# Feed-forward rows transposed by DMA instead of TensorE, in a two-layer recurrent-memory transformer kernel

## The chip, the core and the metric

The kernel runs on one core of a Trainium2 chip. A core has a matrix engine (TensorE, PE in the profile; its weight loads are PEld), three elementwise engines (VectorE or DVE, ScalarE or ACT, GpSimd or POOL) and SyncE (SP), whose queue issues most DMAs. The metric is the device time of one execution in microseconds.

## The reference

The input is one sequence of 2048 rows of 576 numbers. Two layers are applied, and each is attention with a recurrent memory followed by a gated feed-forward; both layers use the same weights.

```python
x = x + _A_ref(_layernorm(x), mem0, Wq, Wk, Wv, Wo, 32)
x = x + _B_ref(_layernorm(x), w1, w3, w2)
# the same two lines once more
def _A_ref(...):            # 64 segments of 32 rows, 32 heads of 128
    for s in range(n_seg):
        h = concatenate([mem, xs])            # 8 memory rows and 32 rows
        q, k, v = h Wq, h Wk, h Wv
        o = softmax(mask(q k^T * scale)) v    # per head
        o = o Wo
        mem = o[:, :8]                        # the next segment needs this
        outs.append(o[:, 8:])
def _B_ref(x):  return (silu(x w1) * (x w3)) w2    # 4608 hidden columns
```

The memory makes the attention of a layer a chain of 64 segments. Layer norm is taken over a row's 576 numbers.

## The kernel before

**Steps and jobs.** A step t works on segment t of layer 0 and on segment t - 8 of layer 1 together, where both exist; there are 72 steps. Four segments make a group of 128 rows. When a group of a layer has gone through attention, a feed-forward job (`job`, L460) takes it: the job of one point in time holds a group of layer 0 and a group of layer 1, two blocks of 128 rows. Its hidden columns are worked in 18 slices, whose weights (W13, W2C) are loaded from memory anew for each job.

**A step on PE.** Queries and keys (QK, and QKt for the last 64 of the 576 numbers), values (VX, VM, VG), scores (SC), the transposed probabilities times the values (PV), and the output projection (WO, WOt). Between scores and PV lie the mask's addition (`sm_add`), the maximum, the exponential on ACT, the sum and the normalised probabilities PB. With both layers at work PB is transposed into PTS by a DMA (`ptr_dma`, L1046, on SP); with one layer, in the first and last eight steps, PE does it (`ptr`). There is one PTS buffer. The last WO tails are spread over two halves of the partitions; `y_odd` (L1112) copies the second half to YO on ACT, and `y_mem` and `yts` add the first half to it, for the next step's memory rows and for YTS, the attention's output with the 576 numbers across partitions.

**A job's entry.** `post_tr` (POST) turns a group of YTS back into rows with five PE transposes, `post_add` adds them to XR on DVE, `ln_nodes` (L277) takes the layer norm: statistics on DVE, the power on POOL, the normalised rows XN on DVE (`ln_norm`, L792). `ln_tr` (L802) transposes XN on PE, each 128 columns as two half-array matmuls, and `xtb_write` (L844) copies the bank to XTB on ACT or DVE. The feed-forward's up matmuls (FF and FFt) read XTB. The same `ln_nodes` serves the attention's inputs (L0tr, L1tr), whose transposes go to HT instead.

**Who sets the order.** PE's order is written out: one letter a PE step, in `FIRST`, eleven times `FOUR`, and `LAST` (L201 to L222). A turn of `FOUR` is four steps and one two-block job. `plan` (L78) walks the steps with assumed durations, follows the letters on PE and places the steps of the other engines and of SP's queue where their inputs and buffers (POOLS, L38: eight PSUM banks among them) let them start. What it decides is the order on each engine; each engine then runs its instructions in that order and waits on semaphores.

**Array divisions.** A PE step uses the array whole (128 x 128), in column halves or quarters (128 x 64, 128 x 32) or in row halves (64 x 128 and smaller). `plan` picks between whole and column halves where a step allows both. The tails of 64 rows (QKt, FFt, VGt and the like) use row halves.

```python
            for c in range(5):
                for r in (0, R64):
                    c0 = min(c * P + r, D - R64)
                    self.mm(self.lnps(b)[r:r + R64, c, :], self.T.XN[:, xn.i, c0:c0 + R64], self.T.ident[:, 0:P], True, True,
                            is_transpose=True, tile_position=(0, r))
```

These are the ten matmuls of `ln_tr`; the tenth block of 64 columns is the ninth again, so that XTB's last block holds the last 64 numbers on both halves of the partitions.

Of the kernel before, what the change touches and what calls it, by code (L numbers as in the profile page):

```python
# [13 lines left out]
P = 128  # L14
# [22 lines left out]
NOW = 1.0e18  # L37
POOLS = {"bank": 8, "qkt": 4, "sme": 2, "pb": 2, "pts": 1, "ot": 4,  # L38
# [157 lines left out]
def ewh(*ns):  # L196
# [5 lines left out]
    "amqQqQQSqqQSqQTQQqqSqQSxXVvPTPTOPOoToPOOooQQqqqqQSQvqSQVqQQqQSTqSPTXPOTOPToxoPOOooQQqqqvaSVQQqqQSQqTQPSqQqOSoTPO"  # L202
    "TPTPOOoooQQQqqqqQSvSVqqqQQQTSQqPTSOPXTOPTxooPOOooQQpQqqVvqqSnQQSFfqFQqfqqQTQSPFTSfWPOOoofTFPFTOPofOoWQqqqqQQSQQS"
    "FFffqVvqqWQQSTFxqffQFPSXWTFfPOTOPoofTOPFOooWVqfqvQQFSQqqQFSQqfqQWTSQqfPFQTfqFPSOTWPOOFoTooffPFOoWQQqqqqQSvQVSFqf"
    "QqQWqqSQTQPTaOPbSOTxxoPXoTXPOOoovqqpQQQSnQFqfqVSFqfqQQQqSPfqFQfOPSWOPFoOfoFoPWOoFQfqqqQQSQfqFFSGqfgqQQQPWQfqqSFG"
    "SfggGPFOOPWoGogfOPFOooWQQqqfaFSVfqqFQQvqfFSQWQfqqFPSQQWqfOSPFFOoPoWOoffFPOoWQqqqqQQbSQGSQqqgqQQSQqgPGSOPGggOPGOo"
    "PooOoQqqqpQpQQSvqqQSnnVqffFFQQPSqfqFQFSPWwffOFOPwWooFPOOooFqffqQQQqqwWSFQQQqfqfFSGSgqqQQgPGwGPWSggfFOGPOwFPOOooo"
    "oWQqfqqQQQfqSFSVvqqfQQFFPWSfqqQwQFSPaffOwWFPOFOPWOwfooooFfqqQQWQqqSQQqqSbQGgqqSQQgPGSGPGggOPOwOPoooOo"
)
FOUR = (  # L210
    "QQppQqqqqQvVSnnSQFqqfqQQFSqffQPFwOSPWFoffPOFOWwPFOoooFfqfqQQQQqqSWGSFqqfgQQQPQgqqwSGSFPGffggFWGPOwOFPOOoooowVqfq"
    "vQQQQqfqWSFSFfqqqQQwWQFPfqfSFwQOPSWFoFPffOOWPwOoooFqqfQQWQSqqqQQaSbQQqgqqGSQgPGSGPGggOPOwOPoooOo"
)
LAST = (
    "QqqqpQQQSnpQQqqqVvSnSQfqFFPqfQOWPSwoFffOPFoOFPwOffWooFQQQqqqFQSqffqFQQqgSWGSQPwQqqgfGSFPFgfgGwOPOGOPWOffooooFQQq"
    "qqFSQQqqqVSvQQwWQSPFqfqQOWoPSwFFPffOOWPwOoooFvfqQQQqqqQSVSFfqqfQFQQqqSPWQwSOPVovWPOwOPoobOoXxvppVqqQQQqqSQQnSnqq"
    "QFQSTfqfqQPFSTOPFTOPWTOPwOooooFfqqfQQQSQQqqqVvTSQFQqffqqFSQPwTWPSFfOFTwPOTWPOOooooFqfqfQQQwSQqxvqfXVWSFQFTQfqqWP"
    "wQSTFQfqfqFPSOTwPWFOffOTFPwOoooWoFfqqvVQQQqfqSQWwSFFQfqqQQSTWPQqqOTSoPTOPwOToboPxOoXqqqQQQpSVvqqqQQnSQFTfSFQPfqq"
    "QOTSFfPwOTFPofTOPFOooowQQfqqqQSQFvfqqVSQFfqQQSqfqQTwPFSTFPOTfXxPOTwPOOooooFVqqfvQQQSQqfqqQSQFqqqQSQTwPFTSOPoffTO"
    "FPwTOPoofOoFQQvqqQSQqqVSQqqqQqQSTQPTSPFOOTffooPFTOPwOoopFffFwnwFffffFFFwFwfffFFFwfffFFwFwfffFFFwffFFwfffFFww"  # L220
# [11 lines left out]
def make_nodes(em, nseg, pools, o=Opt, dma_bw=230e3, load_bw=345e3):  # L232
# [44 lines left out]
    def ln_nodes(tag, src, xn, deps, prio, writes, warm=False):  # L277

        a = node("DVE", 1.16, em.ln_stats(src, xn), deps=deps, prio=prio, acq=[] if src is xn else [xn], name=tag + "stats")
        p_ = node("POOL", 0.45, em.ln_pow(xn), deps=[a], prio=prio, name=tag + "pow")  # L280
        c = node("DVE", 0.43 if src is xn else 0.6, em.ln_norm(src, xn), deps=[p_], prio=prio, name=tag + "norm")
        b = Slot("bank", users=len(writes))
        d = node("PE", 5 * 0.056, em.ln_tr(xn, b, warm), deps=[c], prio=prio, mode="col", acq=[b], rel=[xn], name=tag + "tr")
        out = []
        for wr, cost, more in writes:
            out.append(node("AD", cost, wr(b), deps=[d] + more + out[-1:], prio=prio, rel=[b], name=tag + "wr"))
        return out
# [20 lines left out]
    vx_ev, last_v, pvs = {}, [], {}  # L308

# [45 lines left out]
    def step(t):  # L355
# [17 lines left out]
        for g in range(NG):  # L373
# [27 lines left out]
            if nl == 2:  # L401
                tr = node("DMA", 1.27, em.ptr_dma(t, g, pb, pts), deps=[pbs], prio=pf - 0.02, acq=[pts], name="TR", lat=2.0)
# [31 lines left out]
        yo = node("ACT", actc(c80), em.y_odd(t), deps=wots[3:], prio=t - 0.008, name="Yodd")  # L434
# [10 lines left out]
    def post(li, g):  # L445

        b = banks(1)
        prio = 4 * g + 4 + LAG * li
        d = node("PE", 5 * 0.056, em.post_tr(li, g, b[0]), deps=[d for j in range(4) for d in yx[li, 4 * g + j]] + ([xr_ld[g]] if li == 0 else []),
                 prio=prio, mode="full/col", acq=b, name="POST")  # L450
# [9 lines left out]
    def job(j):  # L460
# [19 lines left out]
        def norm():  # L480
            for (bi, g, half) in reversed(ents):
                pa = post(bi, g)
                wr.extend(ln_nodes("F", xr[g], Slot("xn"), [pa], s0, [((lambda half: lambda b: em.xtb_write(half, b))(half), cost, prev_ff)], last))
# [113 lines left out]
class Emitter:  # L597
# [116 lines left out]
    def load_xn(self, g, xn):  # L714
        return lambda n: (self.dma if g else self.adma)(self.T.XN[:, xn.i, :], self.a.x[g * P:(g + 1) * P, :])
# [57 lines left out]
    def src_ap(self, src):  # L773
        return self.T.XN[:, src.i, :] if src.pool == "xn" else self.T.XR[:, src.i, :]
# [17 lines left out]
    def ln_norm(self, src, xn):  # L792
        def f(n):
            L = self.T.LNS[:, xn.i]
            self.v("tensor_scalar", self.T.XN[:, xn.i, :], self.src_ap(src), L[:, 12:13], L[:, 15:16],
                   op0=ALU.subtract, op1=ALU.mult)
        return f
# [4 lines left out]
    def ln_tr(self, xn, b, warm=False):  # L802

        def f(n):
            for _ in range(10 if warm else 0):
                self.mm(self.bk(b)[:], self.T.ident[:, 0:P], self.T.WO[:, 0, 0:512], True, True)
            for c in range(5):
                for r in (0, R64):
                    c0 = min(c * P + r, D - R64)
                    self.mm(self.lnps(b)[r:r + R64, c, :], self.T.XN[:, xn.i, c0:c0 + R64], self.T.ident[:, 0:P], True, True,  # L810
# [559 lines left out]
```

## Time and profile before

| | us |
|---|---|
| median of three runs (2652.61 to 2658.91) | 2656.71 |
| the profiled execution | 2657.08 |
| its span | 2655.3 |
| PE busy | 2577.3 (97%) |
| DVE busy | 2042.0 (77%) |
| ACT busy | 1226.3 (46%) |
| one turn of the repeated order, from the trace | 152 to 156 |

In the profile a row of a group names the line of the recording helper, the engine, the operation, what it writes and reads, the shape, the count, and then busy time, the mean duration of one in ns, and the idle time of the engine before it with what ended it. L620 is PE's helper, L623 ACT's, L626 DVE's, so the tiles tell the steps apart. "128*64" on a matmul is the part of the array that it uses. A row of the waits gives the total in us, how many, and the longest. A timeline row starts with the start and the duration in us. A matmul's duration covers its way through the array, some 0.2 us, and matmuls overlap; the work is read from the distance of their starts. "->" and "<-" name the tile written and the tiles read.

### The profile page before, as it was taken

The numbers are of one execution on the slowest core, as the hardware profiler recorded it, in microseconds if no ns is written. First come the engines' busy times: TensorE is split into PE (matmuls) and PEld (weight loads), VectorE is DVE, ScalarE is ACT, GpSimd is POOL, SyncE is SP. The second block draws the span as 40 slices with busy tenths as digits, with TensorE's granted clock in tenths as the row PEclk, the third lists the DMA queues.
The fourth block names the chain that finished last, engine by engine and source line by source line (L and its number), as shares of the span: only waits on it lengthen the run. The fifth ranks groups of instructions, "written<-read, shape, count | busy, mean of one in ns | idle before, by whom it ended". The sixth has DMA issues, their size and how long they took to land.

```text
span 2655.3 us, 132788 instructions
## 1 busy us (share of the span) xinstructions
PE 2577.3 (97%) x58915; PEld 2226.7 (84%) x58915; DVE 2042.0 (77%) x5253; ACT 1226.3 (46%) x3636; POOL 334.9 (13%) x399
## 2 busy tenths in 40 slices
PE   5999999999999999999999999999999999999998
PEld 4788888888888888888888888888888888888887
DVE  4787787787787778778777787787878777787876
ACT  2555453443445444444544444454534435454453
POOL 1111110110111011011101101110110111011110
PEclk8999999999999999999999999999999999999999
DMA  9064745665665556556454645645464564454456
GB/s 322 4 175 126 194 104 147 126 136 146 128 141 109 142 133 146 139 125 155 117 135 118 161 128 133 158 117 132 116 154 126 134 162 103 127 124 129 128 167 227
DMA packets 683056, 371.44 MB, mean 140 GB/s; under 512 B 233736, under 2 KB 672656, under 8 KB 681840
## 3 DMA queue, kind: packets, MB, share of 16 engines
q1 hardware_dynamic: 678944, 355.07, 52.9%
q8 instruction: 460, 7.54, 1.2%
q0 software_dynamic: 3024, 6.93, 0.9%
q10 hardware_dynamic: 512, 0.94, 0.2%
q14 instruction: 116, 0.95, 0.1%
HBM read 306.72 MB, written 2.36 MB: 116 GB/s over the span
## 4 chain that ended last, share of the span: by engine, by line
PE 83%; DMA 8%; DVE 5%; issue 1%; ACT 1%; SPq 1%; POOL 0%; ACTq 0%; DVEq 0%; POOLq 0%
PE bank L620 83%; DMA PTS<-PB 6%; DVE V L626 1%; DVE STAT L626 1%; DMA W<-in_B_w_dram 1%; DVE HTT L626 1%; DVE PB L626 1%; DVE SME L626 1%; DMA W<-in_A_Wk_dram 1%; SPq L629 1%; DMA W2C<-in_B_w_dram 1%; POOL PB L1041 0%; DMA WV<-in_A_Wv_dram 0%; DVE XR L626 0%; ACT V L623 0%
## 5 line engine op out<-in xcount | busy, mean ns | idle before, releaser
L620 PEld LDWEIGHTS <-W 128*128 128x128 bf16 (+2 forms) x31872 | 1254.5, 100 | 138.0 <-issue 68.5
L620 PE MATMUL bank<-HT,W 128*128 128x80 bf16 (+3 forms) x23040 | 804.6, 197 | 23.1 <-DMA W<-in_A_Wk_dram 8.7
L620 PE MATMUL bank<-XTB,W 128*64 128x256 bf16 (+5 forms) x8832 | 666.8, 263 | 2.5 <-DMA W<-in_B_w_dram 2.0
L1041 POOL MEMSET PB<- 128x1024 bf16 x288 | 274.1, 952 | 1954.7 <-DMA PTS<-PB 1298.5
L623 ACT ACTIVATE QKT<-bank 128x256 bf16<-128x256 f32 (+4 forms) x1546 | 356.3, 315 | 298.1 <-PE bank L620 287.2
L620 PE MATMUL bank<-OT,WO 128*128 128x80 bf16 (+3 forms) x11520 | 413.8, 198 | 1.2 <-ACT OT L623 0.6
L620 PEld LDWEIGHTS <-WO 128*128 128x128 bf16 (+1 forms) x11520 | 385.2, 102 | 26.4 <-issue 13.5
L623 ACT ACTIVATE V<-bank 64x512 bf16<-64x512 f32 (+1 forms) x583 | 328.9, 584 | 129.7 <-PE bank L620 122.5
L620 PE MATMUL bank<-WV,HT 128*32 128x512 bf16 (+3 forms) x3952 | 376.4, 386 | 1.2 <-DVE HT L626 0.7
L620 PE MATMUL bank<-W2C,HTT 128*64 128x288 bf16 (+1 forms) x3032 | 319.1, 287 | 1.3 <-DMA W2C<-in_B_w_dram 1.1
L623 ACT ACTIVATE HTT<-bank 128x512 bf16<-128x512 f32 (+1 forms) x324 | 175.7, 551 | 274.6 <-PE bank L620 273.4
L623 ACT ACTIVATE OT<-bank 128x320 bf16<-128x320 f32 (+1 forms) x378 | 142.2, 402 | 314.9 <-PE bank L620 312.1
L626 DVE TENSOR_REDUCE STAT<-SME 104x8 f32<-104x320 f32 (+1 forms) x576 | 273.6, 475 | 15.7 <-ACT SME L623 9.6
L626 DVE TENSOR_TENSOR PB<-SME,STAT 40x128 bf16<-40x128 f32 (+4 forms) x912 | 274.9, 335 | 11.0 <-DVE STAT L626 0.7
L620 PEld LDWEIGHTS <-HT 128*32 128x32 bf16 (+3 forms) x3952 | 168.3, 102 | 116.5 <-issue 22.1
L626 DVE SCALAR_TENSOR_TENSOR HTT<-HTT,bank 128x512 bf16<-128x512 bf16 (+1 forms) x324 | 202.0, 624 | 77.7 <-ACT HTT L623 74.5
L620 PEld LDWEIGHTS <-HTT 128*64 128x64 bf16 (+1 forms) x3112 | 227.8, 104 | 38.5 <-issue 3.4
L626 DVE SCALAR_TENSOR_TENSOR XR<-bank,XR 128x288 f32<-128x288 f32 x576 | 244.8, 448 | 18.5 <-PE bank L620 14.1
L626 DVE TENSOR_TENSOR HTT<-HTT,bank 128x512 bf16<-128x512 bf16 (+1 forms) x324 | 203.6, 628 | 30.8 <-DVE HTT L626 0.9
L626 DVE CAST V<-bank 64x512 bf16<-64x512 f32 (+1 forms) x281 | 192.2, 684 | 42.7 <-PE bank L620 36.3
L623 ACT ACTIVATE SME<-SME 104x320 f32<-104x320 f32 (+1 forms) x288 | 135.0, 469 | 148.1 <-DVE SME L626 146.4
L626 DVE CAST QKT<-bank 128x192 bf16<-128x192 f32 (+2 forms) x502 | 136.1, 315 | 75.3 <-PE bank L620 73.4
(58 smaller groups left out, 1426.2 us busy)
## 6 DMA issues: line engine op xcount, KB each, us to landing
W<-in_B_w_dram SPq DMA_DIRECT2D x608, 256.0 KB, 3.6
W2C<-in_B_w_dram SPq DMA_DIRECT2D x304, 288.0 KB, 3.5
W<-in_B_w_dram SPq DMA_DIRECT2D x608, 32.0 KB, 3.8
W<-in_B_w_dram SPq DMA_DIRECT2D x8, 1024.0 KB, 13.1
W<-in_A_Wq_dram SPq DMA_DIRECT2D x9, 512.0 KB, 9.2
WO<-in_A_Wo_dram SPq DMA_DIRECT2D x4, 1152.0 KB, 16.7
XR<-in_A_x_dram POOLq DMA_DIRECT2D x16, 288.0 KB, 3.8
WV<-in_B_w_dram SPq DMA_DIRECT2D x4, 1152.0 KB, 9.3
```

The source lines that it names most:

```text
L620: self.ch("PE", self.nc.tensor.matmul(out, lhsT=lhsT, rhs=rhs, start=start, stop=stop, skip_group_check=True, **k))
L623: self.ch("ACT", self.nc.scalar.activation(*a, **k))
L626: self.ch("DVE", getattr(self.nc.vector, fn_)(*a, **k))
L629: self.ch("SP", self.nc.sync.dma_start(out=out, in_=in_))
L1041: return lambda n: self.ch("POOL", self.nc.gpsimd.memset(self.T.PB[:, pb.i], 0.0))
```

## The change

1. The feed-forward's normalised rows go from XN to XTB by one DMA transpose of 128 x 640 on SP's queue for each block, in place of PE transposes and a copy out of PSUM. The job at the very end keeps the old way. XN becomes 640 columns wide, and `ln_norm` fills the last 64 by a second DVE instruction, a copy. All layer norms make that copy.
2. The remaining PE transposes of XN are five, of whole 128-column blocks, and may use the whole array.
3. YO no longer has a tile. It lies in rows 64 to 127 of the last block of YTS, which held nothing, one piece for each layer, so `y_odd` copies once for each layer; `y_mem` and `yts` swap the halves that they read. POST's fifth transpose takes 64 rows and 64 columns in place of 128.
4. `FIRST`, `FOUR` and `LAST` are new strings, in `plan` the assumed cost of a DMA transpose is 1.02 us (XTB) or 1.27 us (PTS) and 2.1 us until it lands (it was 1.27 and 2.0), and the norm's assumed cost is 0.18 us higher.
5. A way to bring POST's rows by DMA is written (`post_dma`) but every call takes PE.

```diff
@@ -199,25 +200,25 @@
 FIRST = (
-    "amqQqQQSqqQSqQTQQqqSqQSxXVvPTPTOPOoToPOOooQQqqqqQSQvqSQVqQQqQSTqSPTXPOTOPToxoPOOooQQqqqvaSVQQqqQSQqTQPSqQqOSoTPO"
+    "amqQqQQSqqQSTqQQqQqqSQSVXvxPTPTOPToOoPOOooQqqqqQQSQqvSQVqQqQQSTqSPTXPOTOPToxoPOOooQQqqqvqSVQQaQSQTqqqQPSqQOTSoPO"
...
 FOUR = (
-    "QQppQqqqqQvVSnnSQFqqfqQQFSqffQPFwOSPWFoffPOFOWwPFOoooFfqfqQQQQqqSWGSFqqfgQQQPQgqqwSGSFPGffggFWGPOwOFPOOoooowVqfq"
-    "vQQQQqfqWSFSFfqqqQQwWQFPfqfSFwQOPSWFoFPffOOWPwOoooFqqfQQWQSqqqQQaSbQQqgqqGSQgPGSGPGggOPOwOPoooOo"
+    "QQppQqqqVSvQqqqQQSFSffqQFQPqfFOWoPSwFffFPOwOFPWOoooFffqQQQQqqqwSWGSgqqQQQQfqqFPFSSfggGFPGWwOPOgffGOPFOoooFowWvfq"
+    "VqqQQQSQQQqfqqFSFWSPfqQwQFOfqFSPwoWffOPFOwaPWOoooFqqfQQWSqqqQQQbQqgSGSqqQQPgGOSPGggOPGwOPoooOo"
...
+        c = node("DVE", 0.61 if src is xn else 0.78, em.ln_norm(src, xn), deps=[p_], prio=prio, name=tag + "norm")
+        if by_dma:
+            half, more = by_dma
+            return [node("DMA", TR40, em.xtb_dma(half, xn), deps=[c] + more, prio=prio - 2, rel=[xn], name=tag + "d", lat=TRL)]
...
+                xn = Slot("xn")
+                pa = post(bi, g, xn, True)
+                wr.extend(ln_nodes("F", xr[g], xn, [pa], s0, [((lambda half: lambda b: em.xtb_write(half, b))(half), cost, prev_ff)], last,
+                                   None if last else (half, prev_ff)))
...
     def ln_norm(self, src, xn):
+            self.v("tensor_copy", self.T.XN[:, xn.i, D:D + R64], self.T.XN[:, xn.i, D - R64:D])
...
             for c in range(5):
-                for r in (0, R64):
-                    c0 = min(c * P + r, D - R64)
-                    self.mm(self.lnps(b)[r:r + R64, c, :], self.T.XN[:, xn.i, c0:c0 + R64], self.T.ident[:, 0:P], True, True,
-                            is_transpose=True, tile_position=(0, r))
+                self.mm(self.lnps(b)[:, c, :], self.T.XN[:, xn.i, c * P:(c + 1) * P], self.T.ident[:, 0:P], True, True, is_transpose=True)
...
     def y_odd(self, t):
-            self.cp(n, self.T.YO[:, 0:nq], yT[R64:P, 4, :])
+            for i in range(nq // QW):
+                self.cp(n, self.T.YO[i], yT[0:R64, 4, i * QW:(i + 1) * QW])
...
     def post_tr(self, li, g, b):
+            for db in range(5):
+                k = P if db < 4 else R64
+                self.mm(self.bk_bf(b, D)[:, db * P:db * P + k], self.T.YTS[0:k, li, db, :], self.T.ident[0:k, 0:k], True, True, is_transpose=True)
...
+    def tr_dma(self, out, in_):
+        self.ch("SP", self.nc.sync.dma_start_transpose(out=out, in_=in_))
+    def xtb_dma(self, half, xn):
+        return lambda n: self.tr_dma(self.T.XTB[:, half], self.T.XN[:, xn.i])
...
-    T.XN = sp.tile([P, pools["xn"], D], BF, name="XN")
+    T.XN = sp.tile([P, pools["xn"], D + R64], BF, name="XN")
...
-    T.YO = sp.tile([R64, 2 * QW], F32, name="YO")
+    T.YO = [T.YTS[R64:P, i, 4, 0:2 * QW].bitcast(F32) for i in (0, 1)]
```

In the strings Q and q are QK and QKt, S scores, T PE's transpose of PB, P PV, O and o WO and WOt, X, x, V, v, G, g the values, p POST, n the feed-forward's transposes of XN, a and b those of the attention's inputs, F and f the up matmuls, W and w the down matmuls.

## The prediction

> **What bounds the kernel now.** I read the page's head and slices first, then the waits, then PE's order of time, and last the entry of one feed-forward job.
>
> ```profile
> span 2655.3 us, 132788 instructions
> PE 2577.3 (97%) x58915; PEld 2226.7 (84%) x58915; DVE 2042.0 (77%) x5253; ACT 1226.3 (46%) x3636; POOL 334.9 (13%) x399
> PE   5999999999999999999999999999999999999998
> PEclk8999999999999999999999999999999999999999
> ```
>
> TensorE (PE) is busy from end to end at full clock, so the time is PE's own work plus what PE stands still for. The next rows, of PE alone in order of time, show what that work is made of.
>
> ```profile
> 1466.36 1.32 PE L620 MATMUL bank<-HT,W 128*128 128x80 bf16 x32
> 1467.51 0.45 PE L620 MATMUL bank<-PTS,V 128*128 128x80 bf16 x8
> ...
> 1470.53 1.31 PE L620 MATMUL bank<-OT,WO 128*128 128x80 bf16 x32
> 1471.77 0.40 PE L620 MATMUL bank<-QKT 128*64 128x40 bf16 x15
> ```
>
> Both are 32 matmuls of 80 columns. The first gives way to another full-array step after 1.15 us (32 x 36 ns). The second gives way to a step that uses the array in another division (128*64) after 1.24 us: a change of division costs about 0.1 us. Start to start over the whole trace, a full-array matmul takes 25 ns at 40 columns, 36 at 80, 56 at 128, 109 at 256, 123 at 288 and 216 at 512, and matmuls on halves or quarters of the array share that time. With these intervals PE's matmuls need 2371.5 us. The order holds 1325 changes of division; with the median of each kind (104 to 190 ns) they need 170.5 us. The first matmul starts at 12.4 us and the last ends 4.6 us before the end. So PE stands still for 2655.3 - 2371.5 - 170.5 - 12.4 - 4.6 = 96 us: 47 in the part before the repeated order, 29 in its eleven turns (152 to 156 us each), 20 after them. Some 16 us of the 47 are weight loads at the start. The waits say for whom it stands:
>
> ```profile
> PE bank L620 <- DMA PTS<-PB: 19.9, 29, 1.5
> PE bank L620 <- DVE XN L626: 13.1, 3, 12.4
> PE bank L620 <- ACT HT L623: 7.3, 18, 1.6
> PE bank L620 <- DMA W<-in_B_w_dram: 2.0, 5, 1.0
> ```
>
> The largest repeated wait is PV's for the transposed probabilities (PTS), which a DMA brings; the 12.4 us on XN is the start. The feed-forward transposes that the change removes are waited for hardly at all.
>
> ```profile
> L620 PE MATMUL bank<-ident,XN 128*64 128x128 bf16 x640 | 28.8, 222 | 13.1 <-DVE XN L626 13.1
> L620 PE MATMUL bank<-ident,YTS 128*128 128x128 bf16 x150 | 11.4, 220 | 0.0
> ```
>
> The 640 are 64 sets of ten half-array matmuls, 28.5 ns from start to start: 0.285 us a set. 32 sets are the feed-forward's. The nearest row to the new XTB transfer stands among the DMA issues:
>
> ```profile
> PTS<-PB SPq DMA_TRANSPOSE x224, 3.2
> ```
>
> A transpose by DMA lands 3.2 us after its issue (2.9 to 5.2), and its issue holds SP for 1.24 us.
>
> ```profile
> 1143.89 0.72 PE L620 MATMUL bank<-ident,YTS 128*128 128x128 bf16 x10
> 1149.04 0.58 DVE L626 TENSOR_SCALAR XN<-XR,LNS 128x576 bf16<-128x576 f32 x1
> 1150.07 0.72 PE L620 MATMUL bank<-ident,XN 128*64 128x128 bf16 x19
> 1151.11 0.48 DVE L626 COPY XTB<-bank 128x640 bf16<-128x640 bf16 x1
> 1152.13 1.59 PE L620 MATMUL bank<-XTB,W 128*128 128x256 bf16 x13
> ```
>
> This is a job's entry: POST's matmuls end at 1144.61, the second norm 5.0 us later, the transposes follow, and the first feed-forward matmul starts 7.5 us after POST. PE had other work throughout.
>
> **The change part by part.** The base is the profiled execution, 2657.08 us (the span and 1.8 us around it), 0.4 us above the median of the runs.
>
> *PE's streaming.* 31 feed-forward sets go (the last job keeps its own): 31 x 0.285 = -8.8 us. The other 33 sets become five full-array transposes of 56 ns, 0.28 us, no difference. POST's fifth transpose shrinks from 128 to 64 columns: 30 x 0.03 = -0.9. Together -9.7.
>
> *PE's changes of division.* The new order has 1433 against 1325. A turn of the repeated order has 67 against 59: 143.8 + 7.5 = 151.3 us of work becomes 143.2 + 8.3 = 151.5. With each kind at its median the 108 more cost +10.5. At the lower quartile of each kind it is +10.3; at the kinds' means, which contain waits, +22. I take the medians, since the changes of the commonest kinds lie within a few ns of them. So PE's own work does not shrink.
>
> *Waits that the order itself makes.* For each PE step I summed the other engines' steps between it and the PE step that it needs (medians of their groups, 0.2 us for PE's own latency, 0.06 a handover) and set this against the PE work that lies between. Where the sum is longer, PE must stand. Before, this gives 29.0 us (16.6 ahead of the repeated order, 3.5 in it, 8.9 after it); in the new order 32.8 (19.0, 3.5, 10.3). The 3.5 can be held against the trace: there a turn's wait at the memory's hand-over is 0.34 us, 3.7 in eleven. The growth lies mostly ahead of the repeated order, where scores are followed by PE's own transpose: four places with 5.7 us in place of two with 3.2. I take +3.8; the ends are 0 (the queues cover it already) and +8.
>
> *The new transfer on the path.* In the new order 8.86 us of PE work lie between the second POST and the first feed-forward matmul; by the entry shown (5.84 us of work took 5.4) PE gets there 8.4 us after POST. The chain: norm at 5.0 us as before; two copies of 64 columns that fill XN's last block (0.17 each; a 40-column copy took 0.167); the mask's addition (0.49), now placed between the norms, moves the second by 0.3. The second transfer leaves at 5.5 to 5.6 us and lands 2.9 to 3.2 us later, at 8.4 to 8.8. PE waits 0 to 0.4 us; I take 0.25, twelve times: +3.0. The lower end is 0 (XTB has 5 blocks, PTS 8, so it may land sooner), the upper end is PTS's worst landing, 5.2: 2.4 us x 12 = +29. Jobs of one block have 7.1 to 8.3 us of work against a chain of 6.6 and cost nothing; if that cover fails, four of them add some 0.3 us each.
>
> *SP's queue.* 31 issues at 1.24 us make 38 us of SP's time, 2.5 us a turn of 152. Each is moved ahead of the weight loads and the PTS transposes planned after it, and holds them while it waits for the norm. In a turn the next PTS transpose is ready some 10.6 us after POST, the last XTB issue is over by 6.9: nothing stands behind it. Cost 0; without that cover a PTS transpose is late by up to one issue, 1.24 us x 11 = 14.
>
> *DVE, ACT and POOL.* The XTB evacuations go (ACT 17 x 0.70, DVE 15 x 0.48 us), 64 small copies come (DVE 64 x 0.17 = 11 us). At layer 1's norm the copy has cover: from W2 to its transpose lie 4.45 us of PE work, the chain ends at about 3.1. YO is written in two copies of 0.20 us in place of one of 0.233, +0.17 in 56 steps on ACT; the chain from WO's tail over YO to the next queries' tail takes 1.5 us and has at least 1.9 us of PE work beside it. Cost 0; without cover 56 x 0.17 = 9. POOL does what it did.
>
> *PTS.* The slack of the sixteen PTS chains in a turn, reckoned from the same medians, is 1.65 us in the mean against 1.81, with four chains under 0.6 us against three. I leave the waits at their size: 0, between -20 (all of the 19.9 go) and +8 (four tight chains for three, and half as much again).
>
> Sum: 2657.1 - 9.7 + 10.5 + 3.8 + 3.0 = 2664.7 us.
>
> [...]
>
> **The rivals.** *Faster: PTS waits vanish.* The new order may place PV where its landing no longer ends the wait; 19.9 us in 29 waits are there to win. It decides once more than 13 us of them are gone (7.6 of my sum and 5.3 for a measurable gain); with all gone 2664.7 - 19.9 = 2645. For it: these waits are the largest, and SP's queue ahead of them is ordered anew. Against it: the slack above is not larger, and PE's own work leaves nothing else to save.
>
> *Slower still: XTB lands late.* Where weights are in flight PTS took 4.4 us (nine in ten are below) to 5.2. Then each of twelve entries waits 1.4 to 2.2 us in place of 0.25: +14 to +23, 2679 to 2688. For it: W13's loads start at the same time. Against it: at a job's entry few loads are due. [...]
>
> *No difference.* The order's own waits were covered by queues already, and XTB lands in 2.9 us: -9.7 + 10.5, 2658.
>
> **How the numbers follow.** My forecast has 0.46, the vanished PTS waits 0.26, the late XTB 0.14, no difference 0.14. A difference under 0.2% (5.3 us) can hardly be told from none here. The forecast's own range, 2658 to 2672, lies with one part in five inside it. So faster 0.26, same 0.24, slower 0.50. The range reaches to both other cases: 2642 to 2684.
>
> **What would show it.** Right: PE's transposes of XN fall from 640 to 175 matmuls, PE's busy time stays within 5 us of 2577, the first feed-forward matmul of a job waits briefly for DMA XTB<-XN, a turn of the order takes 152 to 156 us as before. Wrong: a wait on XTB of over 1 us a job, or PTS waits under 10 us in all, or a turn under 152 us; each would move the time by the amount of its rival.

## The result, and the profile after

The changed kernel takes 2663.89 us in the median (2658.31 to 2666.77, seven runs) beside 2655.67 us (2650.48 to 2658.91, seven runs) for the kernel before on the same chip: a ratio of 1.0033, 95% interval 1.0023 to 1.0044. It is slower, by 8 to 9 us (8.2 by the medians, 8.8 by the ratio). The prediction was 2664.7 us.

The head of the page and the first of its rows on engines, of the changed kernel:

```profile
span 2662.1 us, 131470 instructions
PE 2582.7 (97%) x58216; PEld 2220.5 (83%) x58216; DVE 2038.0 (77%) x5244; ACT 1243.0 (47%) x3734; POOL 336.2 (13%) x399
```

PE has 699 matmuls fewer and is busy for 5.4 us more than before (2577.3 us). The intervals and prices of the prediction, applied to the new trace, give 2361.6 us of streaming (it was 2371.5), 181.0 us for 1433 changes of division (170.5 for 1325) and a remainder of 103.3 us in which PE stands still (96.4). So the two parts that PE works came out even, +0.6 us, and the remainder grew by 6.9 us. The waits that name the releaser (total in us, how many, longest):

```profile
PE bank L633 <- DMA PTS<-PB: 12.0, 21, 1.1
...
PE bank L633 <- issue: 10.5, 13, 2.7
PE bank L633 <- ACT HT L636: 7.0, 18, 1.6
...
PE bank L633 <- DVE PB L639: 3.8, 5, 1.6
PE bank L633 <- ACT QKT L636: 3.6, 8, 0.8
PE bank L633 <- DMA W2C<-in_B_w_dram: 2.7, 6, 0.6
...
PE bank L633 <- DMA XTB<-XN: 1.7, 4, 0.6
```

The same rows of the kernel before, where they are not in the prediction:

```profile
PE bank L620 <- issue: 8.2, 9, 2.9
...
PE bank L620 <- ACT QKT L623: 1.7, 6, 0.4
...
PE bank L620 <- DMA W2C<-in_B_w_dram: 1.1, 3, 0.5
...
PE bank L620 <- DVE PB L626: 0.4, 2, 0.2
```

The new wait, on XTB, is small. The old one, on PTS, fell from 19.9 to 12.0 us. What grew is spread over rows of 2 to 4 us that were shorter before. Summed over all rows of PE behind the first 14 us, the waits for a DMA fell from 32.4 to 26.2 us, those for another engine rose from 19.0 to 24.4, those that name nobody (issue) from 8.2 to 10.5. That is only 1.5 us more in all. The other 5 us of the remainder are idle stretches under 0.15 us, which the rows leave out, and changes that took longer than the median of their kind. The next two answers are of the tile XTB and of the timeline (start, duration, operation, and in brackets the idle time before it): the same job's entry that the prediction showed, in the new kernel.

```profile
L1180 SPq DMA_TRANSPOSE XTB<-XN x31: 1199/1228/2168, 130.9 to 2519.6; - x31
DMA to landing us min/median/max: 2.6/2.7/4.1
```

```profile
1149.29 0.87 PE L633 MATMUL bank<-ident,YTS 128*128 128x128 bf16 x8
...
1158.61 0.43 PE L633 MATMUL bank<-QKT 128*64 128x40 bf16 x16
1159.52 1.94 PE L633 MATMUL bank<-XTB,W 128*64 128x256 bf16 x32 [0.49 <-DMA XTB<-XN]
```

In a job of two blocks the second transfer is issued 5.35 us after POST where nothing delays it, and lands 2.6 us later, at 7.95 us. PE reaches the first feed-forward matmul at 8.67 us. That is 0.7 us to spare; in the entry shown the second transfer took 3.9 us to land, and PE waited 0.49 us.

### The profile page after: what moved, and what is told of

Same layout as the page of the kernel before. It is cut to its first block, busy times and chain, and to the rows that moved or that the text cites. A ratio compares the mean times of both kernels' runs of the same rounds, so it can differ in the third digit from the quotient of the medians.

```text
span 2662.1 us, 131470 instructions
## 1 busy us (share of the span) xinstructions
PE 2582.7 (97%) x58216; PEld 2220.5 (83%) x58216; DVE 2038.0 (77%) x5244; ACT 1243.0 (47%) x3734; POOL 336.2 (13%) x399
## 4 chain that ended last, share of the span: by engine, by line
PE 86%; DMA 8%; DVE 3%; ACT 1%; issue 1%; SPq 0%; POOL 0%; ACTq 0%; DVEq 0%; POOLq 0%
PE bank L633 86%; DMA PTS<-PB 4%; DMA W<-in_B_w_dram 1%; DMA W2C<-in_B_w_dram 1%; DMA W<-in_A_Wk_dram 1%; DVE V L639 1%; DVE STAT L639 1%; DMA XTB<-XN 1%; ACT QKT L636 1%; DMA WV<-in_A_Wv_dram 0%; ACT V L636 0%; DVE HTT L639 0%; DVE SME L639 0%; DVE XR L639 0%; DVE PB L639 0%
## 5 line engine op out<-in xcount | busy, mean ns | idle before, releaser
L633 PE MATMUL bank<-HT,W 128*128 128x80 bf16 (+3 forms) x23040 | 795.3, 197 | 23.1 <-ACT HT L636 7.0
L636 ACT ACTIVATE QKT<-bank 128x64 bf16<-128x64 f32 (+2 forms) x1638 | 373.9, 314 | 330.6 <-PE bank L633 290.7
L633 PE MATMUL bank<-OT,WO 128*128 128x80 bf16 (+3 forms) x11520 | 420.1, 199 | 2.6 <-issue 1.0
L633 PE MATMUL bank<-WV,HT 128*32 128x512 bf16 (+4 forms) x3592 | 372.2, 384 | 0.0
L633 PEld LDWEIGHTS <-HT 128*32 128x32 bf16 (+4 forms) x3592 | 156.4, 99 | 128.5 <-issue 22.7
L639 DVE CAST V<-bank 32x512 bf16<-32x512 f32 (+1 forms) x272 | 186.0, 684 | 21.0 <-PE bank L633 16.1
L639 DVE CAST OT<-bank 128x320 bf16<-128x320 f32 (+1 forms) x211 | 97.3, 462 | 108.4 <-PE bank L633 95.3
```

Of the source, the lines that this page charges most:

```text
L633: self.ch("PE", self.nc.tensor.matmul(out, lhsT=lhsT, rhs=rhs, start=start, stop=stop, skip_group_check=True, **k))
L636: self.ch("ACT", self.nc.scalar.activation(*a, **k))
L639: self.ch("DVE", getattr(self.nc.vector, fn_)(*a, **k))
```

## The experiments

They ran in four sessions on four chips, on which the kernel before took 2663.8 to 2666.3 us in the median. So ratios to the kernel before of the same session are compared; differences between runs of two sessions are differences of such ratios, and spans and waits of two sessions are set side by side with that reserve. Divisions, streaming and remainder are worked out of each run's trace as above. The one profile of the kernel before from these sessions is the one of the section on the kernel before and the changed kernel; its remainder is 104.7 us.

### One part at a time: order, DMA, the smaller parts

Three kernels, each half of the change. The first keeps the old order and PE's transposes into XTB, and has only the smaller parts (YO in YTS, wide XN with its copy, POST's 64-row fifth transpose, the new assumed durations).

```diff
-FIRST, FOUR, LAST of the changed kernel
+FIRST, FOUR, LAST of the kernel before
...
-                                   None if last else (half, prev_ff)))
+                                   None))
```

> The old order, XTB still transposed by PE; from the change only the smaller parts: YO in YTS, POST's fifth transpose of 64 rows, the wider XN with its copy. My theory (the time is PE's streaming, plus about 0.1 us for each change of division, plus waits): POST's fifth transpose now needs row halves and brings 62 more changes of division (1387 against 1325), +6.6 us, streaming -1.3, waits +0.8: 2655.7 + 6 = 2662 us. Rival (the DMA transposes and what waits for them cost the time, changes of division are hidden): 2656 us, as before.

The second has the whole change, in the old order: the old strings with the feed-forward's n struck out.

> The whole change except the new order: the old letters with the feed-forward's transposes struck out, XTB by DMA. My theory: streaming -9.9 and 61 more changes of division +6.5, but only 7.2 us of PE work lie between POST and the first feed-forward matmul of a two-block job, so PE is there after 6.8 us while the transfer lands at about 8.1 (norm at 5.0, two copies, 2.7 us of landing): 1.3 us x 11, and some 3 us in the one-block jobs: +17; other waits +4. 2655.7 - 3.4 + 21 = 2673 us, with a wait for DMA XTB<-XN of over 1 us in each turn. Rival (the transfer is hidden wherever it stands): 2656 us and no such wait.

The third has the new order with an n put back for each block of each job, and PE's transposes.

> The new order and the smaller parts, but XTB transposed by PE again (the transposes put back into the order where XN is ready, with no further change of division). My theory: 8.7 us more streaming than the changed kernel, 1.7 us of waits for the transfer less: 2663.9 + 7 = 2671 us. Rival (the DMA transposes are what costs): at or below the kernel before, 2656 us or less.

| | XTB by PE | XTB by DMA |
|---|---|---|
| old order, with the smaller parts | 1.0123 (1.0107 to 1.0138) | 1.0234 (1.0220 to 1.0248) |
| new order, with the smaller parts | 1.0075 (1.0062 to 1.0088) | 1.0033 (1.0023 to 1.0044) in the first session, 1.0039 (1.0024 to 1.0054) in a later one |

All three kernels took longer than expected, by 0.2% (the third) to 1.7% (the second). Read as they stand, the four say first: the DMA and the order belong together. In the new order the DMA takes about 0.4% off, 10 us; in the old one it adds 1.1%. The waits of the two kernels in the old order show why, first XTB by PE, then XTB by DMA:

```profile
PE bank L633 <- DMA PTS<-PB: 40.1, 39, 2.4
```

```profile
PE bank L633 <- DMA PTS<-PB: 40.5, 44, 2.8
PE bank L633 <- DMA XTB<-XN: 30.5, 17, 3.2
```

The 30.5 us on XTB are the DMA in the old order, where the first feed-forward matmul comes too early for the transfer: it waits 0.8 to 0.9 us in the turns in which nothing delays the transfer, and up to 3.2 us in others. Second: the new order with the smaller parts, but without the DMA, costs 0.75%, some 20 us, against the kernel before. That is more than the 8.8 us of PE transposes that the DMA takes away. By the trace it is 9.2 us of PE's own work and 8.5 us of remainder (113.2 against 104.7). Third, the smaller parts cost 33 us in the old order, where 6 were to be expected, and doubled the PTS waits. That had no explanation and was followed up. What was found there, 15 us that hang on when blocks of PE's program are fetched, bears on the table too: its four kernels have 3325, 3305, 3286 and 3276 matmuls in a turn, so their fetches fall on different places, and the differences between the fields hold that effect as well as the order and the DMA.

### The kernel before and the changed kernel on one chip

> The kernel before, for its profile on the chip that serves the next three. Its time should stand within 0.3% of the 2655 to 2667 us of the two sessions so far. PE's work and changes of division are the same 2371.5 + 170.5 us by construction; what can differ is the time PE stands still, 96 us in the first profile. If a chip on which everything is about 10 us slower shows some 106 us here, the difference between chips is waiting and not PE's work, and the waits of the variants (139 us with the smaller parts alone, 174 us with DMA in the old order) are to be held against 106.

> The changed kernel beside the others on one chip. My reading: ratio to before 1.002 to 1.004, since PE's own work is equal (2542.0 against 2542.5) and only some 7 us of waits are added. If the 58 divisions that a POST of whole width saves are worth their 6 us, this should stand 0.2% above that variant's 1.0035 ratio, so near 1.0055; if it stands at 1.0033 again, a division saved at POST is given back as waits.

The kernel before has a span of 2663.9 us with a remainder of 104.7, so of the 8.6 us that it takes longer here 8.3 are PE standing still, as expected. The changed kernel: 1.0039 (1.0024 to 1.0054), remainder 115.0, +10.3; waits on XTB are 4.6 us here (7, the longest 1.1). POST at whole width was run in the session of the three kernels above:

```diff
             for db in range(5):
-                k = P if db < 4 else R64
-                self.mm(self.bk_bf(b, D)[:, db * P:db * P + k], self.T.YTS[0:k, li, db, :], self.T.ident[0:k, 0:k], True, True, is_transpose=True)
+                self.mm(self.bk_bf(b, 5 * P)[:, db * P:(db + 1) * P], self.T.YTS[:, li, db, :], self.T.ident[:, 0:P], True, True, is_transpose=True)
```

> The changed kernel, but POST's fifth transpose takes all 128 rows and 128 columns again (it writes 64 columns of the bank that nobody reads), so that it needs no row halves. My theory: 58 changes of division fewer (1375 against 1433), -6.3 us, streaming +1.3: 2663.9 - 5.0 = 2659 us. Rival (changes of division are hidden, streaming counts): 2665 us.

It has 58 changes of division fewer, 5 us by the prediction's prices, and measured 1.0035 (1.0021 to 1.0048). The two intervals are too wide to exclude those 5 us, but nothing of them is to be seen. The next section has the same question the other way round, in the old order.

### Why the smaller parts cost 33 us in the old order

Two kernels take the parts away by steps. One has the durations that the plan assumed before:

```diff
-TR40, TR56, TRL = 1.02, 1.27, 2.1
+TR40, TR56, TRL = 1.02, 1.27, 2.0
...
-        c = node("DVE", 0.61 if src is xn else 0.78, em.ln_norm(src, xn), deps=[p_], prio=prio, name=tag + "norm")
+        c = node("DVE", 0.43 if src is xn else 0.6, em.ln_norm(src, xn), deps=[p_], prio=prio, name=tag + "norm")
...
-        yo = node("ACT", actc(*([QW] * nl)), em.y_odd(t), prio=t - 0.008, name="Yodd",
+        yo = node("ACT", actc(c80), em.y_odd(t), prio=t - 0.008, name="Yodd",
```

> The smaller parts in the old order as in the first run, but with the durations that the plan assumed before (norm 0.43 and 0.60 us, 2.0 us until a transpose lands, one YO copy). That run took 1.0123 where 60 divisions (+6 us) explain 1.002. Theory: the new assumed durations moved DVE's and SP's steps, and with them PTS (waits of 40 us): then this run falls to 1.002 to 1.004. Rival: the parts themselves delay the chain (the 64-column copy stands on DVE before a norm is done, YO is two copies and waits for POST): then it stays at 1.010 to 1.014.

The other has also the narrow XN without copy and the ten half-array transposes, so that only YO's place and POST's 64 rows are left:

```diff
-            self.v("tensor_copy", self.T.XN[:, xn.i, D:D + R64], self.T.XN[:, xn.i, D - R64:D])
...
-                self.mm(self.lnps(b)[:, c, :], self.T.XN[:, xn.i, c * P:(c + 1) * P], self.T.ident[:, 0:P], True, True, is_transpose=True)
+                for r in (0, R64):
+                    c0 = min(c * P + r, D - R64)
+                    self.mm(self.lnps(b)[r:r + R64, c, :], self.T.XN[:, xn.i, c0:c0 + R64], self.T.ident[:, 0:P], True, True,
+                            is_transpose=True, tile_position=(0, r))
```

> The kernel before with YO in YTS's spare rows and POST's fifth transpose of 64 rows, and nothing else: XN is narrow, no 64-column copy, ten half-array transposes. If the copy and the wide XN cost the time, this is 1.002 to 1.004 (the 60 divisions at POST, +6 us). If YO's second copy and its new wait for POST cost it, it is at 1.010 or more.

Measured: 1.0123 with everything, 1.0078 (1.0060 to 1.0095) with the old assumed durations, 1.0002 (0.9991 to 1.0013) without the copy too. Three things follow.

The last kernel has 61 changes of division more than the kernel before, from POST's row halves: +6.9 us of divisions and -1.1 of streaming by the prices. It measures +0.5 us (-2.4 to +3.5). On the spot the changes do cost it: from the matmul before POST to the one behind it, beyond the intervals of the matmuls, a POST of two blocks takes 0.44 us with its four changes and 0.00 us without, and all POSTs together 8.5 us against 2.1. The time is no longer for it, because PE stood still for less elsewhere: the remainder was 100.7 instead of 104.7 us. Which waits gave way isn't shown; those on PTS did not (24.9 us against 20.6).

The assumed durations cost 0.45%, 12 us, by the ratios of two sessions. Only the order on DVE, ACT and POOL differs between the two kernels, not SP's. Followed through the last PV of a turn: the mask's addition starts 2.03 us after the scores with the new durations and 0.79 with the old, PB is begun at 6.51 against 4.35, and PV waits 1.94 us in the mean of eleven turns against 1.47.

The third step, 20 us for a 64-column copy and five transposes in place of ten, was not what it seemed. The same last PV of a turn waits 0.1 us without the copy and 1.47 us with it (the expectation further down has 0.16 and 1.63: it reckons from start to start), although each step up to the issue of the transposition stands at the same distance from the scores in both (TR issued at 6.31 us in most turns). Only the landing differs. PE's rows there, first without the copy, then with it:

```profile
1298.57 1.31 PE L633 MATMUL bank<-OT,WO 128*128 128x80 bf16 x32
1299.95 0.45 PE L633 MATMUL bank<-PTS,V 128*128 128x80 bf16 x8
```

```profile
1310.82 1.31 PE L633 MATMUL bank<-OT,WO 128*128 128x80 bf16 x32
1313.61 0.45 PE L633 MATMUL bank<-PTS,V 128*128 128x80 bf16 x8 [1.48 <-DMA PTS<-PB]
```

and the DMA queues in the 3 us of that transposition, with the copy (queue: packets, MB, share; then the issues with their landing):

```profile
q1 hardware_dynamic: 926, 0.23, 40.1%
q8 instruction: 1, 0.02, 2.0%
...
W2C<-in_B_w_dram SPq DMA_DIRECT2D x2, 288.0 KB, 3.6
PTS<-PB SPq DMA_TRANSPOSE x1, 4.6
```

The two weight loads are issued 1.8 us behind the transposition, and they are issued there without the copy too; the 0.23 MB on q1 are the transposition's own. Apart from its packets there is one packet, of 16 KB, on a queue that the page calls "instruction". Over the whole run that queue reads, first of the changed kernel, then of the kernel before:

```profile
q8 instruction: 455, 7.45, 1.1%
```

```profile
q8 instruction: 460, 7.54, 1.2%
```

58216 matmuls and as many weight loads, divided by 455, are 256 a packet; in the kernel before 58915 matmuls go with 460 packets. In both traces the n-th of these packets, counted from 0, starts when PE has begun 128 n and 25 to 192 more matmuls, from the first packet to the last. From these counts I infer that the packets are PE's program, in blocks of 256 instructions, 128 matmuls with their weights. One starts every 5.8 us, and its median length is 1.05 us in the kernel before and 1.03 us in the changed kernel. (A second queue of that name, q14, has 117 packets of mostly 8 KB; they were not followed up.) In ten traces of this study a PTS transposition lands 2.97 us after its issue (median) where no such block is fetched. Where one starts 0.75 to 1 us after the issue it is 3.95 (88 cases), at 1 to 1.25 us 4.14 (110), at 2 to 2.25 us 4.55 (70). From 2.25 us on it is split: 58 of 136 land after more than 4 us, at 2.5 to 2.75 us 79 of 114, later 9 of 29. XTB's transfer goes from 2.6 us to between 3.3 and 4.4 in the same way. In the kernel with the copy 114 of 198 PTS transpositions have a fetch that starts 0.5 to 2.75 us behind the issue, in the kernel without it 71. The last one of a turn has it 2.5 to 2.7 us behind its issue in all eleven turns with the copy, and lands after 4.5 to 4.7 us; without the copy the fetch starts at 0.6 us or earlier there, or none comes, and it lands after 2.9 to 3.6.

Why the same one each turn? A turn of that kernel has 3325 matmuls, 26 blocks less three; the kernel before has 3330, 26 blocks and two. So the fetches keep their place in the turn, good or bad, for all eleven. The changed kernel has 3276, 26 blocks less 52: its fetches move on by 76 of 128 matmuls from turn to turn and no place is hit always.

### Moving the program fetches

This was an explanation by correlation, so the fetches themselves were moved: 60 tiny matmuls, written to a bank that is overwritten, at 4.7 us, where PE would wait until 12.7 us. The same lines were put into the kernel before.

```diff
     def ln_tr(self, xn, b, warm=False):
         def f(n):
+            if not hasattr(self, "shifted"):
+                self.shifted = True
+                for _ in range(60):
+                    self.mm(self.bk(b)[:, 0:MEM], self.T.ident[:, 0:P], self.T.ident[:, 0:MEM], True, True)
...
```

> The smaller parts in the old order with the old assumed durations, and 60 tiny matmuls (8 columns) on PE at 3.7 us, where PE waits for its first input until 12.7 us anyway. They shift by 60 of 128 matmuls the places at which PE's program is fetched, in blocks of 16 KB (128 matmuls with their weight loads) by the DMA engines. In the traces so far a PTS transpose lands 2.97 us after its issue, and 3.6 to 4.6 us after it where such a block is fetched 0.5 to 2.5 us behind the issue. A turn has 3325 matmuls there, 26 blocks less 3 matmuls, so the same PTS of each turn is hit: the last PV of a turn waits 1.63 us in place of 0.16. Theory (fetch): with the shift its transposes are missed, PE's waits on transposes fall from 40 us to 11 to 19, the ratio from 1.0078 to 0.998 to 1.002. Rival (the 64-column copy's time on DVE, or the wide XN's place in memory): the shift changes nothing, 1.006 to 1.0095.

> The kernel before with the same 60 tiny matmuls in the idle time at the start, nothing else. A turn has 3330 matmuls, 26 blocks and 2, so its fetches too keep their place from turn to turn. Theory (fetch): the waits on transposes rise from 24 us to some 32 to 38, by the traces' landings with each fetch taken 60 matmuls earlier: ratio 1.002 to 1.006. Rival: no effect, 1.000.

The kernel with the copy falls from 1.0078 to 1.0021 (1.0011 to 1.0032): 15 us by work that does nothing, just above the range that was expected. Its answer on the tile PTS and its PE at the same place, before the shift and with it:

```profile
DMA to landing us min/median/max: 2.9/3.5/6.1
```

```profile
DMA to landing us min/median/max: 2.9/3.0/5.6
```

```profile
1299.62 1.31 PE L633 MATMUL bank<-OT,WO 128*128 128x80 bf16 x32
1300.97 0.45 PE L633 MATMUL bank<-PTS,V 128*128 128x80 bf16 x8
```

The wait of 1.48 us is gone; waits on PTS fall from 33.0 to 16.2 us in all. The last transposition of a turn now has its fetch 0.2 to 0.7 us behind the issue and lands after 2.9 to 3.6 us. The hits moved rather than vanished: a PV 27 us into the turn, which hardly waited for PTS before, waits in nine of the eleven turns, up to 1.6 us. Some 5 us (1.0021 against 1.0002; 1 to 9 by the two intervals) are left for the copy, the wide XN and the five whole transposes together, and the rival, their own cost, is out as the main cause.

The kernel before with these lines measures 1.0013 (1.0003 to 1.0022). Expected were 1.002 to 1.006. But the edit did something else there. In the kernel before the step that it stands in uses column halves, and the helper makes two matmuls of each. PE's first row, in the kernel with the copy and in the kernel before:

```profile
4.72 1.74 PE L633 MATMUL bank<-ident 128*128 128x8 bf16 x60 [4.72 <-DVE bank L1359]
```

```profile
4.72 3.36 PE L620 MATMUL bank<-ident 128*64 128x8 bf16 x120 [4.72 <-DVE bank L1334]
```

120 matmuls are a block of 128 less 8, so the fetches came back to within 8 matmuls of their old places: transpositions with a fetch 0.5 to 2.75 us behind the issue went from 69 to 75 of 198, PTS waits from 20.6 to 19.2 us. So the run bears out neither the expectation nor its rival: what half a block's shift does to the kernel before was not tested. The expectation's reckoning for such a shift, 0.2 to 0.6%, is as large as the difference between the kernel before and the changed kernel. How much of that difference hangs on a good place of the fetches in the kernel before stays open. In the traces as they are the changed kernel waits less for DMAs than the kernel before (26.2 against 32.4 us, above), so nothing there points to fetches as what makes it longer.

### An order near the old one, made for the DMA

If the new order is what costs, the old one with each job's first feed-forward step moved a little later might keep the gain. The piece of the repeated order in the diff is the place behind POST. This kernel has XTB by DMA, the old strings without n and with the feed-forward one or two steps later, POST whole, the copy for the feed-forward's norms alone, ten half-array transposes for the attention's, and the old assumed durations.

```diff
-VSSQFqqfqQQFS
+VSSQQFqqfqQFS
```

> XTB by DMA in an order near the old one: the old strings without the feed-forward's n, each job's first feed-forward step moved one or two steps later (8.2 to 8.5 us of PE work behind POST), POST whole, the 64-column copy for the feed-forward's norms alone, ten half-array transposes for the attention's, the assumed durations of before. PE's own work by the intervals: 2363.0 + 170.8 = 2533.8 against 2542.1 us (-8.3); the order's own waits 32.0 against 29.0 (+3). Theory: what the order must give for XTB is about 8.5 us of work, so the 30 us of waits on XTB in the unmoved order go, and the time falls to 0.997 to 1.001 of before; a turn has 3310 matmuls, 18 short of 26 blocks, so the program's fetches drift through the turn and the waits on PTS are those of an average place, some 30 us. Rival: old order and DMA don't go together, SP's queue and the norm's chain cost again what they cost in the unmoved order: 1.01 or more.

It measures 1.0129 (1.0114 to 1.0143): the rival. By count PE has 8.3 us less to do, but the remainder is 140.9 us against 104.7. The waits:

```profile
PE bank L633 <- DMA PTS<-PB: 25.9, 33, 2.2
PE bank L633 <- DMA XTB<-XN: 14.6, 11, 2.5
...
PE bank L633 <- DMA W<-in_B_w_dram: 9.3, 14, 1.6
```

Half of XTB's 30.5 us are gone, half are not. Some 0.7 us less of work lies behind POST than in the new order (8.2 to 8.5 us against 8.9 to 9.3). PE reaches the first feed-forward matmul 8.3 us after POST, and a transfer that no fetch delays lands at 8.1, in time. That is so in three of the eleven turns. In the other eight a block of the program starts with the first issue or up to 2.5 us behind one of the two, and PE waits 0.3 to 1.7 us: the order has no reserve for it. W13's loads, on the same queue, are waited for as well. No kernel of this study is measurably faster than the kernel before.

### What the XTB wait costs when the order has no room

> The changed kernel with each XTB transfer issued twice, the same data to the same place: the block is complete 1.23 us later (one more issue on SP), and SP has 38 us more to issue. Theory: the new order leaves XTB no margin, PE reaches a two-block job's first feed-forward matmul about when the second block lands (waits of 0.2 to 0.4 us a turn there now), so each of twelve entries costs 1.0 to 1.25 us more, +12 to +15 us, and the ratio goes from 1.0039 to 1.008 to 1.010. Rival: the order holds more than a microsecond in reserve and only landings delayed by a program fetch are waited for: 1.004 to 1.006, waits on XTB under 8 us. Either way PTS waits stay where they are if nothing stands behind the transfers on SP (within 5 us of 13.7).

```diff
     def xtb_dma(self, half, xn):
-        return lambda n: self.tr_dma(self.T.XTB[:, half], self.T.XN[:, xn.i])
+        def f(n):
+            for _ in range(2):
+                self.tr_dma(self.T.XTB[:, half], self.T.XN[:, xn.i])
+        return f
```

Measured 1.0449 (1.0430 to 1.0468), far from both. The edit did more than meant: in this trace a second transfer to the same place is issued only when the first has landed, 2.6 us or more behind it, so the last of a job's four transfers lands 14.5 us after POST in place of 8.7 (means of twelve jobs). PE waits 84.8 us on XTB, 5.0 us each. Against the changed kernel that is 80 us; the run is 103 us longer by the spans, of two chips. The rest is in the rows of one entry, PE's timeline and the windows of its first microseconds (window, length, busy time and instructions of PE, PEld, DVE, ACT, POOL, then PE's granted clock, DMA share, GB/s):

```profile
1210.87 3.62 PE L633 MATMUL bank<-XTB,W 128*64 128x256 bf16 x32 [4.59 <-DMA XTB<-XN]
```

```profile
1200.00:1204.00 4.00, 4.00 (x116) 2.97 (x108) 3.74 (x12) 3.65 (x14) 1.02 (x2) 1.00 0.21 41
1204.00:1211.00 7.00, 2.41 (x72) 2.34 (x70) 4.73 (x12) 3.88 (x12) 0.00 (x0) 0.80 0.41 77
1211.00:1214.40 3.40, 3.40 (x38) 3.39 (x38) 0.00 (x0) 0.00 (x0) 0.95 (x1) 0.50 0.30 58
1214.40:1218.00 3.60, 3.60 (x78) 3.27 (x75) 2.39 (x6) 1.85 (x6) 0.00 (x0) 0.91 0.55 158
```

Behind the wait of 4.59 us the clock stays at half for 4.2 us of PE's work: 0.50 through the third window, 0.91 in the mean of the fourth, which is another 0.65 us at half. The 32 matmuls that took 1.94 us in the changed kernel take 3.62. A mean of 0.80 over the 7 us of the second window is 2.8 us at half, so the clock fell some 1.9 us into the wait. About 2 us are lost behind it; as an estimate from this one entry, seventeen such waits lose up to some 35 us, where 23 are to be explained. PTS waits stayed at 12.2 us, so nothing stands behind XTB's transfers on SP even when there are twice as many.

The question of the reserve is answered by the entries of the changed kernel rather than by this run: 0.7 us where no fetch falls into the transfers, and waits of 0.2 to 0.6 us (in the later session 0.3 to 1.1) only where one does. In all eleven such entries of the two traces a block starts 0.5 to 2.3 us behind one of the two issues; it delays the landing or holds the first issue for up to 2.3 us in place of 1.2.

## Why the prediction was right, point by point

**The sum.** 2664.7 us were predicted for a base of 2657.08, +7.6; measured are +8.2 by the medians of one chip. The forecast's own case came out: slower, inside 2658 to 2672. That it came out within a microsecond is in part luck: the terms below missed by up to 8 us, and the misses cancelled. Of the signs, PE's busy time was just missed (2582.7 us, 5.4 over 2577), and the wait on XTB came in four of the job entries only.

**PE's streaming, -9.7.** The trace has -9.9. The transposes of XN fell from 640 matmuls to 175 as counted.

**PE's changes of division, +10.5.** The number was right, 1433. Two things about it were not. The prediction put it down to the new order; 58 of the 108 come from POST's fifth transpose, which with 64 rows works in row halves (with POST whole the new order has 1375), and 50 from the order. And adding their price to the time does not hold for POST's: the kernel with 61 changes more was no slower (+0.5 us, -2.4 to +3.5, where 5.8 were due), although POST itself took 6.4 us longer there. The price is right on the spot; what failed is the step from there to the sum, as if no wait elsewhere gave way. "PE's own work" and "waits" can't be added up more finely than some 6 us.

**The order's own waits, +3.8, and XTB's, +3.0.** Their sum, 6.8, met the remainder's growth of 6.9 us, but by another way. Summed by kind of step, the remainder fell by 13 to 14 us at PV and rose at SC (6 to 7), at the feed-forward's up steps (5 to 8), at W2 and WO (5 to 7) and at PE's own transposes of PB (2.9). The split over the other steps hangs on the price that each kind of change is given, and nothing rests on it. In the eleven turns the remainder is 28.8 us before and after; the growth lies ahead of them (+3.9) and behind (+2.8), where the prediction had it in smaller sizes (+2.4 and +1.4, XTB aside).

**XTB's term.** It was sized at 3.0 us for twelve jobs; measured are 1.7, and 4.6 in the later session. Norm and issue came as worked out (5.35 us after POST against 5.5 to 5.6), PE arrives at 8.67 (8.4), but the transfer lands in 2.6 us and not in 2.9 to 3.2; five blocks land sooner than eight (medians of 2.7 and 3.0 us in this trace), which the prediction had as its lower end. What waits there are, are the fetch's, a cause that was not in the prediction. So the size came out near for another reason than the one given.

**SP's queue, DVE, ACT, at nothing.** SP: right by PTS's waits, also with 62 transfers. DVE and ACT: right within some 5 us (1.0021 against 1.0002) for the copy, in the old order; YO's second copy costs nothing that can be measured there (1.0002, 0.9991 to 1.0013).

**PTS, 0.** Wrong in the direction of the faster rival: the row fell from 19.9 to 12.0 us, the remainder at PV by 14. The rival asked for 13 us, and by PV alone it had them, but it took for granted that nothing else would be given back. That PE came to the next steps earlier and waited there fits the rows of the other engines, but no run shows it. Fewer hits by a fetch are not the reason for the fall: 74 of 198 PTS transpositions have a fetch 0.5 to 2.75 us behind the issue, 64 had before.

**The other rivals.** The late XTB came true in the old order (30.5 us in 17 waits), not in the new one. Its reason, weights in flight, does not come out of the trace of the kernel before: without a fetch PTS lands after 2.98 us with weight loads in flight and 2.92 without, and in 35 of the 36 landings over 4 us a block of the program starts between 1 us before the issue and the landing. The order that makes room for the transfer is what the change pays with: 20 us with the smaller parts, of which the DMA returns 10, both with the reserve that no run holds the fetches' places fixed.

## What to carry to other kernels

When PE is busy from end to end, taking work off it pays only if the order that the replacement needs is no dearer; run the new order without the new mechanism, and the mechanism in the old order, and the two prices can be told apart, as far as they exceed what a shift of the program's fetches does. Before a slowdown of under 1% is put down to an edit, see whether the landings of the DMAs on the path moved with the number of instructions: sixty matmuls at an idle place were worth 15 us here. Then count in the trace what such a shift really issued; the same lines gave 60 matmuls in one kernel and 120 in the other. Behind the one wait of 4.6 us that was looked at, PE lost some 2 us more at half the clock.

## What the runs showed of the hardware that was not expected

DMA transpositions landed later where a packet of the queue "instruction" started behind their issue. Such a packet, of 16 KB and about 1.05 us long, comes every 5.8 us. Where one starts 0.75 to 2.25 us behind the issue, a PTS transposition lands 1.0 to 1.6 us later than the 2.97 us without one (medians of 3.95 to 4.55 us), and at 2.5 to 2.75 us 79 of 114 land after more than 4 us. With 3325 matmuls in a repeated turn, 3 less than a multiple of 128, the same transfer is hit in each of eleven turns; 60 matmuls more at an idle place moved that kernel from 1.0078 to 1.0021 of the time of the kernel before. That a block belongs to PE is inferred from the counts, 256 instructions a packet and 128 matmuls on average from one start to the next; which of the DMA engines it shares with the transposition wasn't looked into.
